# First two token tiles: attention in 128-query blocks instead of 64-query blocks

## The chip, the cores and the metric

The kernel runs on one core of one Trainium2 chip. The core has five engines with queues of their own: TensorE (PE), VectorE (DVE), ScalarE (ACT), GpSimd (POOL) and SyncE (SP), and 16 DMA engines that move data between HBM and the core's SBUF. The metric is the device time of one execution in microseconds.

## The reference

```python
# attention, q k v: (4 batches, 8 heads, 768 positions, 64); mem_k mem_v: (4, 8, 8, 64); chunk 32
for c in range(24):
    k_full = concat([mem_k, k[:, :, max(0, 32*c-16):min(768, 32*c+40)]])      # 8 memory rows + at most 56 rows
    s = q[:, :, 32*c:32*c+32] @ k_full.T / 8
    a = exp(s - max(s)); a = a / (sum(a) + 1e-9)
    out[:, :, 32*c:32*c+32] = a @ v_full                                      # the same rows of v
x = out as (3072 tokens, 512)                                                 # heads side by side
h = x @ w_in;   y = maximum(0.01*h, h) @ w_out                                # w_in 512x2048, w_out 2048x512
h = y @ w_in2;  out = P(h) / (Q(h) + 1e-6) @ w_out2                           # P cubic, Q quadratic
```

The weights arrive as float64, the rest as float32.

## The kernel before

The 3072 tokens go through both layers in six tiles of 512 tokens. A layer's tile is a loop over 16 items `f` of 128 hidden columns: a group of 12 matmuls `hps` (L597: four slices of the contraction times three products of high and low parts), an activation on ACT with a subtraction on DVE (L607 to L610), and a group of 12 matmuls `acc` (L655 in the first layer, L693 in the second). `advance_h` runs `hps` two items ahead of `acc`.

The first layer's weights are loaded and converted while its first tile runs. A half (128 columns of `w_in` or 128 rows of `w_out`, 512 KB as float64) goes through one of three `wr` buffers: `load_w` (SP), `scale_w` (ACT, L133), `join_w` (three DVE instructions, L147 to L154; the last one frees the buffer), `split_w` (ACT, L165) and the low part (DVE, L168). `weights0` does one step of each, twice per item.

Attention of a tile has to be done before that tile's first `hps`. Tiles 2 to 5 use the `wide_*` functions: blocks of 128 queries, transposed by DVE and by DMA through HBM, while matmuls of earlier tiles run. The first two tiles have other functions, `att_*`, with blocks of 64 queries and TensorE for every transpose: `att_a` transposes q (every second block) and k and copies both out of PSUM on ACT; `att_b1` makes the scores and their maximum; `att_e` is the exponential; `att_b2` divides by the sum; `att_c` transposes the probabilities and copies them out in four pieces; `att_d` multiplies by v and splits the result into `xh` and `xl`. The eight blocks of the first tile run at the start, with nothing beside them but loads and the first weights; the exponential follows a subtraction on DVE (L311). The eight blocks of the second tile are put by `attend` into the items of the first tile's first layer; there the exponential takes the maximum as bias and gives the sum (L324).

The order on each engine is the order of the calls in the source: the program is recorded under `tc.manual_schedule()`, and an engine does its instructions in that order. Semaphores are added between engines. A PSUM bank, an SBUF buffer or a DMA semaphore that is used again makes the new user wait for the old one; loads on SP and ACT share eight DMA semaphores in turn, so a load is issued only when the load eight places before it has landed. `psw` is a ring of four PSUM banks for `hps` and attention, `psa` four banks for `acc`, lent to attention during the start.

Of the kernel before, what the change touches and what calls it, by code (L numbers as in the profile page):

```python
# [9 lines left out]
F32 = mybir.dt.float32  # L10
# [7 lines left out]
QB = 64  # L18
# [6 lines left out]
def kernel(  # L25
# [31 lines left out]
    CTX = QB + LCTX + RCTX  # L57
# [4 lines left out]
    assert WIN == SB and QB == 2 * CHUNK  # L62
# [145 lines left out]
    NB = sum(n for _, n in tiles_of[0][:WIDE_FROM]) // QB  # L208
    BPS = S // QB
    tile_of = {}  # L210
    for i, (s0, n) in enumerate(tiles_of[0][:WIDE_FROM]):
        for j in range(s0 // QB, (s0 + n) // QB):
            tile_of[j] = (i, j * QB - s0)

    FIRST = tiles_of[0][0][1] // QB
    spare = [xpool.tile([P, KC, NMAX], F32R, tag=t, name=t) for t in ("xh", "xl")]  # L220
    room = [t[:, n, :].bitcast(F32).rearrange("p (h d) -> p h d", h=H) for t in spare for n in range(KC)]
    rooms = {"k": [kb[0], kb[1]] + room[0:2], "v": [vb[0], vb[1]] + room[2:4], "q": room[4:8]}

    def place(kind, j):
        return j % (4 if j < FIRST else NKV)

    qr, qT, kT, pm = {}, {}, {}, {}
    in_mem = {}

    def load_kv(j, src, mem, kind, spans):  # L230
        bi, blk = divmod(j, BPS)
        t = rooms[kind][place(kind, j)]
        c0 = blk * QB - LCTX
        for row, at, n, is_mem in spans:
            if is_mem:
                if in_mem.get((kind, place(kind, j), row)) != bi:
                    in_mem[kind, place(kind, j), row] = bi
                    nc.sync.dma_start(out=t[row:row + n], in_=mem[bi].rearrange("h p d -> p h d"))  # L238
            else:
                lo, hi = max(c0 + at, 0), min(c0 + at + n, S)  # L240
                row += lo - c0 - at
                nc.sync.dma_start(out=t[row:row + hi - lo], in_=src[bi, :, lo:hi, :].rearrange("h p d -> p h d"))  # L242

    def load_q(j):
        bi, blk = divmod(j, BPS)
        t = rooms["q"][j // 2] if j < FIRST else raw.tile([P, H, D], F32, tag="qr", name="qr", bufs=1)
        nc.sync.dma_start(out=t, in_=q[bi, :, blk * QB:blk * QB + P, :].rearrange("h p d -> p h d"))
        qr[j] = t

    def load_k(j):  # L250
        load_kv(j, k, mem_k, "k", ((0, 0, NM, True), (NM, 0, CTX, False), (NM + CTX, 0, NM, True)))

    def load_qk(j):
        if j >= NB:
            return
        if j % 2 == 0:
            load_q(j)
        load_k(j)

    def load_v(j):  # L260
        if j < NB:
            W = WIN - NM
            load_kv(j, v, mem_v, "v", ((0, 0, NM, True), (NM, 0, W, False),
                                       (SB, CHUNK, W, False), (SB + W, 0, NM, True)))

    def att_bank(j, name):

        if j < FIRST:
            return psa.tile([P, 512], F32, tag="acc", name=name)
        return psw.tile([P, 512], F32, tag="ps", name=name)  # L270

    def att_a(j):
        if j % 2 == 0:
            t = qr.pop(j).rearrange("p h d -> p (h d)")
            ps = psw.tile([P, 512], F32, tag="ps", name="psq")
            for p in range(NP):
                nc.tensor.transpose(ps[:, p * P:(p + 1) * P], t[:, p * P:(p + 1) * P], ident)
            o = tmp.tile([P, NP, P], F32, tag="A", name="qT")
            nc.scalar.mul(out=o.rearrange("p c m -> p (c m)"), in_=ps, mul=scale)
            qT[j] = qT[j + 1] = o  # L280
        t = rooms["k"][place("k", j)].rearrange("p h d -> p (h d)")
        ps = psw.tile([P, 512], F32, tag="ps", name="psk")
        for p in range(NP):
            nc.tensor.transpose(ps[:, p * KW:(p + 1) * KW], t[:KW, p * P:(p + 1) * P], ident[:KW, :KW])
        o = tmp.tile([P, NP, KW], F32, tag="kT", name="kT", bufs=1)
        nc.scalar.copy(out=o.rearrange("p c m -> p (c m)"), in_=ps[:, :NP * KW])
        kT[j] = o

    def att_b1(j):
        blk = j % BPS  # L290
        ps = psw.tile([P, 512], F32, tag="ps", name="pss")[:, :NP * WIN].rearrange("p (c m) -> p c m", c=NP)
        qt, kt = qT.pop(j), kT.pop(j)
        qo = (j % 2) * QB
        for p in range(NP):
            for e in range(2):
                r = slice(e * 64, e * 64 + 64)
                for c in range(2):
                    o = e * 64 + c * CHUNK
                    nc.tensor.matmul(ps[o:o + CHUNK, p, :], qt[r, p, qo + c * CHUNK:qo + (c + 1) * CHUNK],  # L299
                                     kt[r, p, c * KOFF:c * KOFF + WIN], start=True, stop=True)  # L300
        for e in range(2):
            if blk == 0:
                nc.vector.memset(ps[e * 64:e * 64 + CHUNK, :, NM:NM + LCTX], NEG)
# [62 lines left out]

    NCH = P // CHUNK
# [503 lines left out]
```

## Time and profile before

| | us |
|---|---|
| median of 3 runs (1160.58 to 1161.16) | 1160.8 |
| span of the profiled execution, first to last instruction | 1158.6 |
| first `hps` matmul starts (end of the start) | 47.07 |
| first scores of tile 2 on TensorE, in item 14 of the first tile | 156.79 |
| PE busy | 1132.9 (98%) |
| DVE, ACT, POOL busy | 776.2, 637.2, 223.2 |

The page gives the span of the profiled execution and no other time for it; the median of the runs is 2.2 us above that span. In the rows below "busy" of PE is modelled from issue to end of pipelined matmuls, so two matmuls issued 0.23 us apart can each last 0.39 us. In a timeline, the start of the next row is therefore the better measure of what a group costs its engine. `<-` after a bracket names what ended the wait before a row. Shapes with `f32` are float32 matmuls, which the trace records as two instructions each where the operand is not an identity.

### The profile page before, as it was taken

What the parts mean: (1) busy time and instruction counts of PE and PEld (TensorE: products, weight loads), DVE (VectorE), ACT (ScalarE), POOL (GpSimd) and SP (SyncE); (2) the same over time, 40 slices, a digit from 0 to 9 for tenths busy, and PEclk for the clock granted to TensorE, in tenths of its full rate; (3) what the DMA queues carried; (4) which work ended last, traced back from release to release, by engine and by line L of the source; (5) the groups of instructions that cost most, each with busy time, mean ns of one, the idle gap of its engine ahead of it and who ended that gap; (6) DMA issues with size and microseconds to landing.
All of it is one profiled execution on the core that took longest, in us unless ns stands there. A gap on an engine that the chain in (4) does not pass through costs nothing.

```text
span 1158.6 us, 19707 instructions
## 1 busy us (share of the span) xinstructions
PE 1132.9 (98%) x7552; PEld 927.0 (80%) x7552; DVE 776.2 (67%) x1388; ACT 637.2 (55%) x1195; POOL 223.2 (19%) x255
## 2 busy tenths in 40 slices
PE   6799999999999999999999999999999999999998
PEld 4577778888888888888888888888888888888887
DVE  3788865564555645543344888788788788788775
ACT  4677642332233223232345877777777777777765
POOL 0000111232121321130000222222222222222222
PEclk7899999999999999999999999999999999999999
DMA  8677787778777678753342200200200200200001
GB/s 175 165 199 194 182 239 192 204 223 256 205 194 240 195 214 235 200 161 102 99 144 73 92 1 1 73 1 1 73 1 1 73 1 1 73 1 1 37 1 37
DMA packets 148592, 132.00 MB, mean 114 GB/s; under 512 B 63415, under 2 KB 119063, under 8 KB 148499
## 3 DMA queue, kind: packets, MB, share of 16 engines
q1 hardware_dynamic: 143635, 123.30, 37.8%
q0 software_dynamic: 4864, 7.45, 2.7%
q8 instruction: 60, 0.98, 0.4%
q14 instruction: 33, 0.27, 0.1%
HBM read 92.93 MB, written 37.75 MB: 113 GB/s over the span
## 4 chain that ended last, share of the span: by engine, by line
PE 93%; ACT 2%; DMA 2%; DVE 1%; SPq 1%; issue 1%; ACTq 0%; DVEq 0%
PE hps L597 45%; PE acc L693 23%; PE acc L655 22%; PE psx L507 2%; PE pss L465 1%; DMA kb<-in_k_dram 1%; ACT pb L347 1%; SPq L238 1%; DMA wr<-in_moe_w_in_dram 0%; DMA qr<-in_q_dram 0%; SPq L242 0%; PE psx L354 0%; DVE ww L150 0%; PE pss L299 0%; ACT pm L324 0%
## 5 line engine op out<-in xcount | busy, mean ns | idle before, releaser
L633 POOL TENSOR_TENSOR gl<-R,gh 128x512 fp32r<-128x512 f32 x96 | 124.4, 1296 | 503.3 <-ACT gh L632 460.9
L607 ACT ACTIVATE gh<-hps 128x512 fp32r<-128x512 f32 x96 | 57.5, 599 | 295.3 <-PE hps L597 295.2
L610 DVE TENSOR_TENSOR gl<-s,gh 128x512 fp32r<-128x512 f32 x96 | 66.4, 691 | 183.4 <-ACT s L608 180.2
L597 PE MATMUL hps<-xh,wih 128*128 128x512 f32 x384 | 154.1, 401 | 0.9 <-ACT xh L363 0.5
L655 PE MATMUL acc<-gh,woh 128*128 128x512 f32 x384 | 151.4, 394 | 0.0
L597 PE MATMUL hps<-xh,wil 128*128 128x512 f32 x384 | 150.4, 392 | 0.4 <-DVE wil L168 0.4
L597 PE MATMUL hps<-xl,wih 128*128 128x512 f32 x384 | 150.3, 392 | 0.0
L655 PE MATMUL acc<-gh,wol 128*128 128x512 f32 x384 | 149.7, 390 | 0.0
L655 PE MATMUL acc<-gl,woh 128*128 128x512 f32 x384 | 149.5, 389 | 0.0
L693 PE MATMUL acc<-woh,gl 128*128 128x512 f32 x384 | 149.4, 389 | 0.0
L597 PE MATMUL hps<-yh,wih 128*128 128x512 f32 x384 | 149.4, 389 | 0.0
L693 PE MATMUL acc<-woh,gh 128*128 128x512 f32 x384 | 149.4, 389 | 0.0
L597 PE MATMUL hps<-yl,wih 128*128 128x512 f32 x384 | 149.4, 389 | 0.0
L693 PE MATMUL acc<-wol,gh 128*128 128x512 f32 x384 | 149.4, 389 | 0.0
L597 PE MATMUL hps<-yh,wil 128*128 128x512 f32 x384 | 149.4, 389 | 0.0
L430 POOL DMA_DIRECT2D vb<-in_v_dram x128 | 83.7, 655 | 258.3 <-PE psx L507 202.0
L620 ACT ACTIVATE A<-hps 128x512 f32<-128x512 f32 x96 | 57.1, 595 | 113.9 <-PE hps L597 113.8
L636 DVE SCALAR_TENSOR_TENSOR A<-A,small,pb 128x512 f32<-128x512 f32 x96 | 72.0, 750 | 56.5 <-ACT pb L621 56.4
L597 PEld LDWEIGHTS hps<-xh,wih 128*128 128x128 f32 x384 | 72.4, 189 | 17.7 <-ACT xh L363 0.7
L627 DVE SCALAR_TENSOR_TENSOR A<-A,pb 128x512 f32<-128x512 f32 x96 | 66.4, 692 | 30.1 <-ACT pb L640 30.1
L597 PEld LDWEIGHTS hps<-xh,wil 128*128 128x128 f32 x384 | 72.4, 188 | 16.2 <-DVE wil L168 0.8
L655 PEld LDWEIGHTS acc<-gh,wol 128*128 128x128 f32 x384 | 72.1, 188 | 15.5 <-DVE wol L168 0.3
(102 smaller groups left out, 2018.7 us busy)
## 6 DMA issues: line engine op xcount, KB each, us to landing
wr<-in_moe_w_in_dram SPq DMA_DIRECT2D x32, 512.0 KB
wr<-in_moe_w_out_dram SPq DMA_DIRECT2D x32, 512.0 KB
park_dram<-pb SPq DMA_DIRECT2D x16, 512.0 KB
pb<-park_dram SPq DMA_DIRECT2D x64, 128.0 KB
w_dram<-ww SPq DMA_DIRECT2D x32, 256.0 KB
wb<-w_dram SPq DMA_DIRECT2D x32, 256.0 KB
vb<-in_v_dram POOLq DMA_DIRECT2D x118, 56.0 KB, 3.6
kb<-in_k_dram SPq DMA_DIRECT2D x59, 112.0 KB
```

What stands on the lines that cost most here:

```text
L238: nc.sync.dma_start(out=t[row:row + n], in_=mem[bi].rearrange("h p d -> p h d"))
L430: nc.gpsimd.dma_start(out=vw[r + at:r + at + n, c], in_=v[bi, hs, lo:lo + n, :].rearrange("h p d -> p h d"))
L507: nc.tensor.matmul(ps[hh][e * 64:e * 64 + 64, i, c * CHUNK:(c + 1) * CHUNK], vw[r, c, 2 * i + e, :], pt[r, c, 2 * i + e, :], start=True, s ...
L597: nc.tensor.matmul(ps[:, :n], w_[:, ws], x_[:, kk, :], start=(kk == 0 and m == 0), stop=(kk == KC - 1 and m == 2))
L607: nc.scalar.activation(out=gh, in_=ps, func=AF.Prelu, alpha=0.01)
L610: return [lambda: nc.vector.tensor_tensor(out=gl, in0=s, in1=gh.bitcast(F32), op=ALU.subtract)]
L620: nc.scalar.activation(out=A, in_=ps, func=AF.Square)
L627: nc.vector.scalar_tensor_tensor(out=A0, in0=A0, scalar=ONE, in1=U0, op0=ALU.add, op1=ALU.mult)
L633: nc.gpsimd.tensor_tensor(out=gl, in0=R0, in1=gh.bitcast(F32), op=ALU.subtract)
L636: nc.vector.scalar_tensor_tensor(out=A, in0=A, scalar=babs[:, 1:2], in1=U, op0=ALU.mult, op1=ALU.add)
L655: nc.tensor.matmul(acc[i][d][:, :n], w_[:, ws], g_, start=(f == 0 and m == 0), stop=(f == FC - 1 and m == 2))
L693: nc.tensor.matmul(acc[i][s], g_[:, ss], w_, start=(f == 0 and m == 0), stop=(f == FC - 1 and m == 2))
```

## The change

The 64-query functions go. The first two tiles get functions of their own for blocks of 128 queries, four blocks per tile:

- `mid_a` transposes q (4 transposes) and two 64-query windows of k (4 each) and copies them out in three ACT instructions. The second window has a PSUM bank of its own.
- `mid_s` makes the scores of all eight heads into two banks, even heads and odd heads, in the same loop as `wide_s`.
- `mid_p` transposes four slabs of 128x128 and copies them out in one ACT instruction instead of eight for two blocks.
- `mid_x` multiplies by v with contraction over 64 rows instead of 128: 32 matmuls of 32 columns for 128 queries instead of 16 of 64 columns. v lies as it does for the later tiles, heads 0 to 3 in rows 0 to 63 and heads 4 to 7 in rows 64 to 127. `weighted` is the loop of `wide_x`, now shared.
- v of a block comes in 8 loads of 56 KB instead of 4 of 112 KB for the same queries. The first block's v is issued from ACT, memory rows of all later k and of all v from POOL.
- There are three rooms for k and v (two in spare `xh`, `xl` buffers); from the fourth block on all use room 0. The first four q blocks lie in spare weight buffers.
- `plan` puts a block of the second tile into six half-items (two per item): transposes of the probabilities of the block before and of q and k in the first, weighted sum of the block before and scores in the second, then the exponential and the division.

```diff
-    def att_c(j):
-        t, _ = pm.pop(j)
-        t = t.rearrange("p (i h) m -> p i (h m)", h=2)
-        ps = att_bank(j, "pst")[:, :NP // 2 * P]
-        for i in range(NP // 2):
-            nc.tensor.transpose(ps[:, i * P:(i + 1) * P], t[:, i, :], ident)
-        ...
+    room = [(kw, vflat), (spare[0][:, 0], spare[0][:, 1]), (spare[1][:, 0], spare[1][:, 1])]
+    def home(j):
+        return j if j < len(room) else 0
+    def mid_load_v(j):
...
+        eng = nc.sync if j else nc.scalar
...
+        for hh in range(2):
+            hs = slice(4 * hh, 4 * hh + 4)
+            for odd in range(2):
...
+                for n in range(2):
...
+                    eng.dma_start(out=t[row + lo - a0:row + hi - a0, odd, n],
+                                  in_=v[bi, hs, lo:hi, :].rearrange("h p d -> p h d"))
+    def mid_p(j):
+        t, _ = mm.pop(j)
+        t = t.rearrange("p e (i h) m -> p (e i) (h m)", h=2)
...
+        for n in range(4):
+            nc.tensor.transpose(ps[:, n * P:(n + 1) * P], t[:, n, :], ident)
+        nc.scalar.copy(out=pwT, in_=ps)
+    def weighted(j, vt, weight, bank):
+        ps = [bank(j, "psx")[:, :2 * P].rearrange("p (i m) -> p i m", i=2) for hh in range(2)]
+        for i in range(2):
+            for c in range(NCH):
+                for hh in range(2):
+                    r = slice(hh * WIN, hh * WIN + WIN)
+                    for e in range(2):
+                        nc.tensor.matmul(ps[hh][e * 64:e * 64 + 64, i, c * CHUNK:(c + 1) * CHUNK],
+                                         vt[r, c, 2 * i + e, :], weight(r, c, i, e), start=True, stop=True)
...
+        for j in range(FIRST, LAST):
+            u = 1 + 6 * (j - FIRST)
+            if j > FIRST:
+                put(u, lambda j=j: mid_p(j - 1))
+            put(u, lambda j=j: mid_a(j))
+            if j > FIRST:
+                put(u + 1, lambda j=j: mid_x(j - 1), lambda j=j: mid_load_v(j))
+            put(u + 1, lambda j=j: mid_s(j))
+            if j + 1 < LAST:
+                put(u + 1, lambda j=j: mid_load_q(j + 1), lambda j=j: mid_load_k(j + 1))
+            put(u + 2, lambda j=j: mid_e(j))
+            put(u + 3, lambda j=j: mid_n(j))
...
+        mid_x(1)
+        load_w(FC * 2)
+        weights0()
+        mid_a(3)
+        mid_n(2)
+        mid_load_q(FIRST)
+        mid_load_k(FIRST)
+        mid_s(3)
+        mid_p(2)
+        mid_e(3)
+        mid_x(2)
+        weights0()
+        mid_n(3)
+        mid_p(3)
+        mid_x(3)
```

Three places show how the instructions move; line numbers with `+` are those of the changed kernel.

On ACT, at the end of the start before, the third half of the weights (`wr_350`) is scaled ahead of the copy of the last k block:

```order
L363 CAST xh_284<-psx_461 128x4x64
L165 CAST wih_474<-ww_352 128x512
L133 ACTIVATE ww_477<-wr_350 128x512
L286 COPY kT_510<-psk_505 128x416
L319 ACTIVATE pm_83<-pm_83 128x256
```

After the change the third half is `wr_362`, and behind its scaling stand the copies of q and both k windows of the last of four blocks:

```order
L387 CAST xh_348<-psx_440 128x2x128
L387 CAST xh_348<-psx_441 128x2x128
L164 CAST wih_480<-ww_241 128x512
L132 ACTIVATE ww_483<-wr_362 128x512
L299 ACTIVATE qT_496<-psq_491 128x512
L307 COPY pb_82<-psk_498 128x416
L307 COPY pb_82<-psk_504 128x416
```

In both the scaling stands directly ahead of the last k copies; what is behind it is an eighth of the tile's attention before and a quarter now.

On SP before, the loads around that third half (`xh` holds v of blocks 6 and 7 here):

```order
L121 DMA wr_350<-in_moe_w_in_dram 128x4x256
L242 DMA xh_85<-in_v_dram 56x8x64 x2
L124 DMA wr_412<-in_moe_w_out_dram 128x1024
L242 DMA xh_85<-in_v_dram 56x8x64 x2
L121 DMA wr_483<-in_moe_w_in_dram 128x4x256
```

The same place after the change (`xl` is v of the third block, `vb` that of the fourth):

```order
L285 DMA xl_86<-in_v_dram 56x4x64 x8
L247 DMA q0_175<-in_q_dram 128x8x64
L262 DMA kb_80<-in_k_dram 88x8x64 x2
L285 DMA vb_81<-in_v_dram 56x4x64 x8
L120 DMA wr_362<-in_moe_w_in_dram 128x4x256
L123 DMA wr_478<-in_moe_w_out_dram 128x1024
```

The third half has moved behind all of the first tile's v.

On PE in the second tile, between two `hps` and `acc` groups, before (of the groups of twelve, one row stands at each end):

```order
L655 MATMUL acc<-gh,wol 128x512
L342 MATMUL pst<-ident,pm 128x128 x2
L299 MATMUL pss<-kT,qT 32x64 x16
L354 MATMUL psx<-pb,vb 64x64 x8
L597 MATMUL hps<-xh,wih 128x512
```

And after, the transposes in one gap:

```order
L637 MATMUL acc<-gh,wol 128x512
L364 MATMUL pst<-ident,t 128x128 x4
L297 MATMUL psq<-ident,qr 128x128 x4
L306 MATMUL psk<-ident,kb 128x104 x8
L579 MATMUL hps<-xh,wih 128x512
```

Behind that group of twelve, in the next gap, stand the weighted sum of the block before and the scores:

```order
L579 MATMUL hps<-xh,wil 128x512
L379 MATMUL psx<-pm,vb 64x32 x32
L320 MATMUL pss<-pb,qT 32x64 x32
L637 MATMUL acc<-gh,woh 128x512
L637 MATMUL acc<-gl,woh 128x512
```

A block of 128 queries now stands in two gaps between groups of twelve; two blocks of 64 stood in five or six.

## Rows read from the trace of the kernel before

**Rows 1.** Windows by stage: PE, PEld, DVE, ACT, POOL busy, PEclk, DMA share, GB/s.
```profile
0.00:47.07 47.07, 27.93 (x449) 21.60 (x449) 26.27 (x73) 24.15 (x68) 1.59 (x7) 0.78 0.72 155
47.07:156.79 109.72, 106.92 (x820) 84.49 (x820) 92.06 (x184) 74.65 (x206) 10.06 (x16) 0.99 0.77 200
156.79:1158.60 1001.81, 998.03 (x6285) 820.91 (x6284) 657.88 (x1132) 538.40 (x922) 211.56 (x232) 1.00 0.35 103
```

**Rows 2.** Windows of shorter stretches, the same columns; the last is GB/s.
```profile
0.00:13.22 13.22, 7.44 (x105) 5.77 (x109) 4.01 (x14) 4.63 (x9) 1.59 (x7) 1.00 0.72 166
0.00:34.00 34.00, 21.61 (x346) 16.90 (x346) 15.33 (x45) 15.49 (x42) 1.59 (x7) 0.80 0.87 185
...
40.00:44.00 4.00, 2.11 (x20) 1.52 (x20) 3.17 (x10) 2.60 (x10) 0.00 (x0) 0.50 0.07 26
...
200.00:250.00 50.00, 49.98 (x515) 40.55 (x514) 29.07 (x71) 14.40 (x29) 11.31 (x18) 1.00 0.76 208
```

**Rows 3.** Timeline of SP: start, duration, the second load of a weight half.
```profile
13.22 0.39 SPq L121 DMA_DIRECT2D wr<-in_moe_w_in_dram  x1
```

**Rows 4.** Timeline of PE in the start: start, duration, group [wait before it].
```profile
24.80 1.12 PE L354 MATMUL psx<-pb,vb 128*64 128x64 f32 x16
25.85 1.08 PE L299 MATMUL pss<-kT,qT 64*32 64x64 f32 x32
...
40.50 0.66 PE L342 MATMUL pst<-ident,pm 128*128 128x128 f32 x2 [3.36 <-DVE pm L335]
41.09 1.12 PE L354 MATMUL psx<-pb,vb 128*64 128x64 f32 x16
```

**Rows 5.** Groups by line and shape, ACT and DVE: busy us, mean ns | idle before.
```profile
L133 ACT ACTIVATE ww<-wr 128x512 f32<-128x512 f32 x63 | 42.7, 680 | 5.4 <-DMA wr<-in_moe_w_out_dram 3.0 <-DMA w_dram<-ww 2.0 <-DMA wr<-in_moe_w_in_dram 0.4
L286 ACT COPY kT<-psk 128x416 f32<-128x416 f32 x16 | 8.1, 507 | 9.0 <-PE psk L284 9.0
L363 ACT CAST xh<-psx 128x256 fp32r<-128x256 f32 x16 | 6.0, 373 | 4.7 <-PE psx L354 4.6
L279 ACT ACTIVATE qT<-psq 128x512 f32<-128x512 f32 x8 | 4.8, 599 | 10.9 <-PE psq L277 10.9
...
L487 DVE TENSOR_TENSOR t<-t,sm 128x512 f32<-128x512 f32 x16 | 11.1, 692 | 0.6
```

**Rows 6.** DVE timeline: first row of one weight half, first row of the next.
```profile
69.03 0.42 DVE L147 TENSOR_SCALAR ww<-ww 128x512 uint32<-128x512 uint32 x1
...
71.42 0.42 DVE L147 TENSOR_SCALAR ww<-ww 128x512 uint32<-128x512 uint32 x1
```

**Rows 7.** The chain of waits, pieces in order: start, us to the next, what.
```profile
47.07 9.84 PE hps L597 x36
...
108.59 0.44 PE psq L277 x4
109.03 0.36 PE psk L284 x4
...
112.17 0.22 PE pst L342 x2
112.39 2.76 PE hps L597 x12
115.15 0.58 PE pss L299 x32
115.73 0.61 PE psx L354 x16
116.34 2.96 PE acc L655 x12
```

**Rows 8.** The same chain at the later tiles' scores and weighted sums.
```profile
156.86 0.79 PE pss L465 x53
...
183.37 2.72 PE hps L597 x12
186.09 1.30 PE psx L507 x64
```

More of the change, by code (lines that the diff above doesn't have):

```diff
@@ L207 @@
     xt = {}
[L208 to L242, printed above, removed]
@@ L260, in load_v @@
[L260 to L303, printed above, removed]
-            if blk == BPS - 1:
-                o = e * 64 + CHUNK
-                nc.vector.memset(ps[o:o + CHUNK, :, WIN - NM - RCTX:WIN - NM], NEG)
-        mx = tmp.tile([P, NP, 1], F32, tag="mx", name="mx")
-        nc.vector.tensor_reduce(out=mx, in_=ps, op=ALU.max, axis=AX.X, negate=True)
-        if j < FIRST:
-            t = mall[:, j % 2]
-            nc.vector.tensor_tensor(out=t, in0=ps, in1=mx.to_broadcast([P, NP, WIN]), op=ALU.add)
-            pm[j] = (t, None)
-        else:
-            pm[j] = (ps, mx)
@@ new lines, in mid_bank, with mid_a @@
+    def mid_bank(j, name):
+        if j < FIRST:
+            return psa.tile([P, 512], F32, tag="acc", name=name)
+        return psw.tile([P, 512], F32, tag="ps", name=name)
+    def mid_a(j):
+        t = mq.pop(j)
+        ps = psw.tile([P, 512], F32, tag="ps", name="psq")
+        for p in range(NP):
+            nc.tensor.transpose(ps[:, p * P:(p + 1) * P], t[:, p * P:(p + 1) * P], ident)
+        o = tmp.tile([P, NP, P], F32, tag="A", name="qT")
+        nc.scalar.mul(out=o.rearrange("p c m -> p (c m)"), in_=ps, mul=scale)
+        mqT[j] = o
+        t = room[home(j)][0]
+        for n in range(2):
+            ps = psw.tile([P, 512], F32, tag="ps", name="psk")[:, :NP * KW]
+            for p in range(NP):
+                f = n * H * D + p * P
+                nc.tensor.transpose(ps[:, p * KW:(p + 1) * KW], t[:KW, f:f + P], ident[:KW, :KW])
+            nc.scalar.copy(out=kwT[:, n * NP * KW:(n + 1) * NP * KW], in_=ps)
@@ new lines, in mid_e @@
+    def mid_e(j):
+        t, ps, mx = mm[j]
+        sm = None
+        if j < FIRST:
+            nc.scalar.activation(out=t, in_=t, func=AF.Exp)
+        else:
+            sm = tmp.tile([P, 2, NP, 1], F32, tag="sm", name="sm", bufs=3)
+            for e in range(2):
+                for p in range(NP):
+                    nc.scalar.activation(out=t[:, e, p, :], in_=ps[e][:, p, :], func=AF.Exp, bias=mx[:, e, p, :],
+                                         accum_out=sm[:, e, p, :])
+        mm[j] = (t, sm)
@@ new lines, in mid_n @@
+    def mid_n(j):
+        t, sm = mm[j]
+        t = t.rearrange("p e n m -> p (e n) m")
+        if sm is None:
+            sm = tmp.tile([P, H, 1], F32, tag="sm", name="sm", bufs=3)
+            nc.vector.tensor_reduce(out=sm, in_=t, op=ALU.add, axis=AX.X)
+        else:
+            sm = sm.rearrange("p e n m -> p (e n) m")
+        nc.vector.tensor_scalar_add(sm, sm, 1e-9)
+        nc.vector.reciprocal(out=sm, in_=sm)
+        nc.vector.tensor_tensor(out=t, in0=t, in1=sm.to_broadcast([P, H, WIN]), op=ALU.mult)
@@ new lines @@
+        for j in (1, 2):
+            mid_load_q(j)
+            mid_load_k(j)
+            mid_load_v(j)
+            if j == 1:
+                load_w(FC * 2)
+        mid_load_q(3)
+        mid_a(0)
+        mid_load_k(3)
+        mid_s(0)
+        mid_e(0)
+        scale_w(FC * 2)
+        mid_a(1)
+        mid_n(0)
+        mid_s(1)
+        mid_p(0)
+        mid_e(1)
+        mid_x(0)
+        mid_load_v(3)
+        load_w(FC * 2)
+        join_w(FC * 2)
+        scale_w(FC * 2)
+        mid_a(2)
```

270 lines of the change are left out of this document (108 added, 162 removed).

## The prediction

> **What bounds the kernel now.** I read the windows by stage first, then the chain of waits, then the timelines of the stages that the change touches. The windows cut the span in three [rows 1]. From 156.79 us on, PE is busy 998.03 of 1001.81 us and none of its instructions change, so I carry that stage over whole. From 47.07 to 156.79 us the first tile's matmuls run with the second tile's attention between them: PE 106.92 of 109.72 us, and DVE, which converts the weights, 92.06. Up to 47.07 us the first tile's attention runs alone, and PE is busy 27.93 us only: there the end is set by loads (185 GB/s over the first 34 us, then 26 GB/s at 40 to 44 us [rows 2]) and, after them, by a ladder of handovers between PE, ACT and DVE, as in the 3.36 us that PE waits for the division at 40.50 us [rows 4]. So the change has two prices, one for each of the first two stages, and they need not have the same sign.
>
> **The start: removed and added.** ACT and DVE save work: two blocks of 64 need eight copies of probabilities, one block of 128 one copy of 512 columns, which I take as the q copy's 0.60 us [rows 5]. That saving lies on engines busy about half of this stage [rows 1], and is worth nothing by itself. What counts is when the last block starts and how long its ladder is.
>
> When it starts. In the changed order ACT scales the third weight half directly ahead of the last block's q and k copies, and SP issues that half behind all of v. In the order before, two of the eight v blocks were still behind the third half. I count what is loaded up to and with it: q 1024 KB, k 1376, v 1760, memory rows 384, three halves 1536, together 6080 KB (6.23 MB); before, 5504 KB. The start moves 185 GB/s [rows 2], so 6.23 MB are through at 33.7 us at the earliest. Landing lags: the first weight half and what was issued ahead of it are 1840 KB (1.88 MB), the load that has to wait for it goes out at 13.22 us [rows 3], and by then 13.22 x 166 = 2.19 MB had moved [rows 2]. With those 0.31 MB (1.7 us) added the third half lands at 35.4 us. I take 35.0, nearer to the measured lag; bounds 33.7 and 38, the upper for a queue that runs dry between the small loads.
>
> How long the ladder is from there. PE's granted clock was 0.50 at 40 to 44 us [rows 2], after PE had waited 3.36 us, and the last block meets the same: PE has nothing to do while ACT waits for the weight. At that level (1.2 GHz) the weighted sum took 1.05 us (24.80 to 25.85) [rows 4] against 0.61 at the full one [rows 7], a factor 1.72. Steps, in order: scaling 0.68, q copy 0.60 and two k copies of 0.51, less 0.3 for their overlap, 2.0 [rows 5]; scores 0.79 x 1.72 = 1.36 [rows 8]; transposes of the third block's probabilities, two pairs of 0.59, 1.18 [rows 4]; their copy 0.60; the third block's weighted sum 1.30 x 1.72 = 2.24 [rows 8]; `xh` 0.37 [rows 5]; two low parts on DVE, of 256 columns like `xh` and taken at its 0.37, 0.74; then, ahead of the last division on DVE, one weight half, 71.42 - 69.03 = 2.39 [rows 6]; the division 1.75 (sum and multiplication at 0.69 each [rows 5], two short ones); transposes 1.18, copy 0.60, weighted sum 2.24, `xh` 0.37. That is 17.0, and 17.3 with a dozen handovers. At the full clock the three weighted sums and scores and the transposes shrink by 3.8 in all: 13.5.
>
> So `hps` starts at 35.0 + 17.3 = 52.3 us instead of 47.07: **+5.2**. Ends: 33.7 + 13.5 = 47.2 (+0.1) and 38 + 17.3 = 55.3 (+8.2).
>
> The loads come in smaller pieces: v in 56 KB instead of 112 KB. The later tiles also load v in 56 KB pieces, and at 200 to 250 us 208 GB/s moved beside them [rows 2], so I charge nothing for the size; if I am wrong it is inside the bound of 38. The Trainium skill, "DMA: Bandwidth & Descriptors", section "Bandwidth", says the opposite: transfers under 64 KB are mostly overhead, with 138 GB/s given for 64 KB. By that figure, as an estimate, the 1.80 MB of v would take 13.0 instead of 9.7 us, and the start would come out 3.3 us later still.
>
> **The stage behind it.** PE's transposes are the same in number (4 of q, 8 of k, 4 of probabilities for 128 queries), on both sides at the same rows [rows 7]: nothing. Scores for 128 queries go from 2 x 0.58 [rows 7] to 0.79 [rows 8], weighted sums from 2 x 0.61 to 1.30: -0.29 a block, -1.2 for four. The weighted sum has twice the matmuls at half the columns and gains nothing by it.
>
> Gaps: a group of twelve takes 2.72 us undisturbed [rows 8], 2.96 behind scores and weighted sum and 2.76 behind a transpose [rows 7], so a gap costs 0.14 on average. I count 22 gaps before and 10 after: -1.7.
>
> Stalls: 31 groups of 2.72 are 84.3; the first three lose 9.84 - 8.16 = 1.7 to the half clock, which I keep; eight blocks cost 4 x 0.44 + 8 x (0.36 + 0.22 + 0.58 + 0.61) = 15.9; 22 gaps 3.1. Of 109.7 that leaves 4.7 us of stalls, in which PE waits for ACT and DVE. ACT loses seven of its eight copies of probabilities a block, DVE one of two multiplications and two short instructions, so they should shrink; but they won't vanish: the second bank of the scores is the bank of the `hps` group just before it, and the next `hps` needs the bank whose low part DVE has still to read. I take 2.5 of 4.7: -2.2. Ends: all gone, -4.7, and 2 us more than before, +2.0.
>
> Together -1.2 - 1.7 - 2.2 = **-5.1**, between -7.6 and -0.9.
>
> **Sum.** 1158.6 + 5.2 - 5.1 = 1158.7 us of span; the median of the runs shown is 2.2 us above the span of the profiled execution, so 1160.9. Both terms are sure in sign and I trust neither to better than 2 us; that they cancel is chance.
>
> **Rivals.** First, the start loses little (faster): the third half lands at 34 us and the clock is back at full in the middle of the ladder; 34 + 15 = 49, +2; with the stage at -6 the time is 1156.8. For it: the mean granted clock of the start is 0.78 [rows 1], so PE was at the full level for a good part of it. Against: 0.50 at 40 to 44 us, in the stretch most like the new ladder [rows 2, 4].
>
> Second, DVE sets the stage's pace (slower). It is busy 92.06 of 109.72 us now; with about as much in a stage of 104.6 it would be 88%. Its order has the low parts of the weighted sum, on which a PSUM bank waits, behind four or five weight instructions, and the eight exponentials on ACT in one piece stand ahead of the weight's high part that DVE's next low part needs. If DVE falls behind PE by more than the slack that `hps` has on that bank, a few tenths of a us, every block pays: then only scores and gaps stay, -1.5 with the stalls 1.4 longer, and the time is 1160.8 + 5.2 - 1.5 = 1164.5. It decides as soon as PE waits over 1.5 us a block. For it: before, PE already waited for ACT and DVE. Against: the PE windows show 97% busy [rows 1].
>
> Third, the loads run dry (slower): the third half lands at 38 us; +8.2 - 5.1, so 1163.9. Only eight loads are out at a time, and eight of 56 KB are 448 KB, 2.4 us at 185 GB/s: about a landing's lag. Against: the pieces are mixed with loads of 176 to 512 KB. The skill's rule above would end here, by its own figure at about 1164.
>
> **Chances.** Forecast (both terms within 2 us of mine) 0.45, first rival 0.27, second 0.16, third 0.12. A change of 0.2% (2.3 us) is about what a measurement of this kernel can tell. Of the forecast's 0.45, 0.33 lie within it, 0.06 on either side; of the first rival 0.22 are faster, 0.05 within; of the second 0.12 slower and 0.04 within; of the third 0.1 slower, 0.02 within. So faster 0.28, same 0.44, slower 0.28. Forecast's own range 1158 to 1164; the range for 8 in 10 is 1155.5 to 1166.
>
> **What would show it.** Right: ACT waits at the scaling ahead of the last q copy, for the DMA of the third half, until about 35 us; first `hps` near 52 us; granted clock 0.5 around 40 to 50 us; first later-tile scores about 104 to 105 us after the first `hps`, with half as many groups of 2.9 us. Wrong: `hps` before 49 us, or the stage as long as before, or PE waits in it for PSUM banks of `psx` and `pss` of over 1 us a block. If the time from the first later-tile scores to the end differs from 1001.8 by over 1 us, the premise that the rest is untouched has failed.

## The result

| | before | after |
|---|---|---|
| median | 1160.7 us (4 runs) | 1167.6 us (4 runs, 1166.9 to 1169.4) |
| span of the profiled execution | 1158.6 | 1167.6 |
| first `hps` | 47.07 | 57.10 |
| from there to the first scores of the third tile | 109.72 | 108.89 |
| from there to the end | 1001.81 | 1001.61 |

The change makes the kernel slower: the ratio of the times is 1.0065, 95% interval 1.0051 to 1.0079, 6.9 us between the medians. The profiled execution is the longest of its four (1169.4), so the 9.0 us between the two spans is some 2 us more than the typical loss. They split as 10.0 in the start, -0.8 in the stage behind it (from the first `hps` to the first scores of the third tile) and -0.2 in the rest. The windows by stage answer to [rows 1], those of shorter stretches to [rows 2] (same columns; PEclk, DMA share and GB/s stand last):

```profile
0.00:57.10 57.10, 29.55 (x577) 23.09 (x577) 23.20 (x57) 17.60 (x35) 18.31 (x38) 0.84 0.69 149
57.10:165.99 108.89, 103.99 (x948) 84.91 (x948) 90.72 (x173) 68.87 (x179) 15.06 (x26) 0.97 0.69 190
165.99:1167.60 1001.61, 997.70 (x6285) 820.59 (x6284) 657.73 (x1132) 538.46 (x922) 214.15 (x235) 1.00 0.35 103
0.00:34.00 34.00, 19.68 (x366) 14.90 (x367) 12.11 (x32) 10.99 (x21) 18.31 (x38) 1.00 0.83 162
25.00:35.00 10.00, 8.05 (x150) 6.45 (x149) 5.84 (x14) 3.89 (x8) 0.00 (x0) 1.00 0.77 141
40.00:45.00 5.00, 2.67 (x68) 1.87 (x68) 1.33 (x4) 2.12 (x5) 0.00 (x0) 0.50 1.04 273
```

In the start the loads moved 162 GB/s over 34 us where [rows 2] had 185, and the DMA engines were busy 0.83 of it. In the stage PE is busy 104.0 us instead of 106.9, and the time is still there: PE waits more.

**The start.** SP's timeline after the change (start, duration; x8 is a row of eight loads), then ACT's and PE's:

```profile
22.44 4.84 SPq L285 DMA_DIRECT2D xl<-in_v_dram  x8
27.58 0.39 SPq L247 DMA_DIRECT2D q<-in_q_dram  x1
28.09 2.10 SPq L262 DMA_DIRECT2D kb<-in_k_dram  x2
30.29 5.83 SPq L285 DMA_DIRECT2D vb<-in_v_dram  x8
36.16 0.40 SPq L120 DMA_DIRECT2D wr<-in_moe_w_in_dram  x1
```

```profile
40.47 0.66 ACT L132 ACTIVATE ww<-wr 128x512 f32<-128x512 f32 x1 [5.67 <-DMA wr<-in_moe_w_in_dram]
```

```profile
31.66 2.03 PE L379 MATMUL psx<-pm,xh 64*64 64x32 f32 x64 [0.73 <-ACT pm L365]
...
42.07 1.62 PE L320 MATMUL pss<-pb,qT 64*32 64x64 f32 x64 [6.02 <-ACT pb L307]
43.62 1.11 PE L364 MATMUL pst<-ident,t 128*128 128x128 f32 x4
45.47 2.03 PE L379 MATMUL psx<-pm,xl 64*64 64x32 f32 x64 [0.73 <-ACT pm L365]
52.89 1.09 PE L364 MATMUL pst<-ident,t 128*128 128x128 f32 x4 [5.39 <-DVE t L357]
54.71 2.03 PE L379 MATMUL psx<-pm,vb 64*64 64x32 f32 x64 [0.73 <-ACT pm L365]
57.10 0.80 PE L579 MATMUL hps<-xh,wih 128*128 128x512 f32 x1 [0.36 <-ACT xh L387]
```

The third weight half goes out at 36.16 us, behind eight loads that took 5.83 us to issue. ACT waits 5.67 us for it, PE 6.02 us behind ACT. Then the ladder runs 16.6 us, with 5.39 us in it in which PE waits for a division.

This execution is the latest of its kind. Six of the kernels below (experiments 7 to 10, 12 and 13) start in the same order. In their profiles ACT scales that half at 37.5 to 40.2 us, and the first `hps` stands at 54.2 to 56.8, in each 16.6 us behind the scaling. So the start costs 7 to 10 us by execution, the 10.0 above are the high end, and what varies is when the half lands.

**The stage behind.** PE's rows at its three long waits:

```profile
110.60 1.23 PE L306 MATMUL psk<-ident,kb 104*128 104x104 f32 x8
112.80 0.50 PE L579 MATMUL hps<-xh,wih 128*128 128x512 f32 x1 [0.97 <-ACT pm L365]
...
132.32 0.94 PE L306 MATMUL psk<-ident,kb 104*128 104x104 f32 x8
134.23 0.50 PE L579 MATMUL hps<-xh,wih 128*128 128x512 f32 x1 [0.97 <-ACT pm L365]
...
150.43 0.63 PE L364 MATMUL pst<-ident,t 128*128 128x128 f32 x4 [2.83 <-DVE t L357]
```

The step from `psk` to `hps` takes 2.20 and 1.91 us at these places, 0.66 at the first block (71.41 to 72.07). What ACT did before it copied the probabilities (`pm`), and what SP did before that:

```profile
109.55 0.69 ACT L132 ACTIVATE ww<-wr 128x512 f32<-128x512 f32 x1 [2.88 <-DMA wr<-in_moe_w_in_dram]
...
112.19 0.56 ACT L365 COPY pm<-pst 128x512 f32<-128x512 f32 x1
```

```profile
97.93 4.49 SPq L285 DMA_DIRECT2D vb<-in_v_dram  x8
102.46 0.67 SPq L247 DMA_DIRECT2D qr<-in_q_dram  x1
103.17 1.05 SPq L262 DMA_DIRECT2D kb<-in_k_dram  x2
104.33 1.11 SPq L120 DMA_DIRECT2D wr<-in_moe_w_in_dram  x1
```

Eleven loads in a row, 6.3 us, stand ahead of a weight half; ACT waits for the half; the copy of the probabilities is queued behind it, with four more ACT instructions between; PE's bank behind the copy. At the second place ACT's wait for the half is 2.75 us. The third wait, for the last block's division (L357), has weight instructions ahead of it on DVE:

```profile
148.56 0.68 DVE L167 TENSOR_TENSOR wol<-ww,woh 128x512 fp32r<-128x512 f32 x1
...
149.59 0.69 DVE L357 TENSOR_TENSOR t<-t,sm 128x512 f32<-128x512 f32 x1
```

I summed PE's timeline of the stage by kind of group, from the first row of a group to the first of the next (a wait counts with the group before it):

| us | hps | acc | psq | psk | pss | pst | psx | sum |
|---|---|---|---|---|---|---|---|---|
| before | 50.43 | 40.39 | 1.73 | 3.40 | 5.05 | 2.49 | 6.23 | 109.72 |
| after | 50.43 | 41.82 | 1.73 | 5.46 | 3.47 | 1.70 | 4.28 | 108.89 |

Scores (`pss`), transposes of probabilities (`pst`) and weighted sums (`psx`) became 4.3 us cheaper; `psk` and `acc`, which the new waits are counted with, became 3.5 us dearer. The equal sums of `hps` hide one more loss: the first three groups took 11.15 us (57.10 to 68.25) where before they took 9.68 (47.07 to 56.75), since PE stayed longer at the half clock, and the other `hps` groups gained as much.

### The profile page after: what moved, and what is told of

Same layout as the page of the kernel before. It is cut to its first block, busy times and chain, and to the rows that moved or that the text cites. A ratio compares the mean times of both kernels' runs of the same rounds, so it can differ in the third digit from the quotient of the medians.

```text
span 1167.6 us, 20228 instructions
## 1 busy us (share of the span) xinstructions
PE 1131.2 (97%) x7808; PEld 928.6 (80%) x7808; DVE 771.6 (66%) x1361; ACT 624.9 (54%) x1135; POOL 247.5 (21%) x298
## 4 chain that ended last, share of the span: by engine, by line
PE 91%; DMA 3%; ACT 2%; DVE 2%; issue 1%; SPq 1%; ACTq 0%; DVEq 0%
PE hps L579 44%; PE acc L675 22%; PE acc L637 20%; PE psx L379 2%; DMA wr<-in_moe_w_in_dram 1%; PE pss L475 1%; ACT t L343 1%; DMA xl<-in_k_dram 1%; DVE ww L149 1%; DMA xh<-in_v_dram 0%; DMA vb<-in_v_dram 0%; SPq L262 0%; ACT ww L132 0%; DVE wol L167 0%; PE pst L364 0%
## 5 line engine op out<-in xcount | busy, mean ns | idle before, releaser
L602 ACT ACTIVATE A<-hps 128x512 f32<-128x512 f32 x96 | 57.1, 595 | 114.0 <-PE hps L579 114.0
L579 PEld LDWEIGHTS hps<-xl,wih 128*128 128x128 f32 x384 | 72.8, 190 | 14.6 <-DVE xl L388 0.2
```

What stands on the lines that cost most here:

```text
L579: nc.tensor.matmul(ps[:, :n], w_[:, ws], x_[:, kk, :], start=(kk == 0 and m == 0), stop=(kk == KC - 1 and m == 2))
L602: nc.scalar.activation(out=A, in_=ps, func=AF.Square)
```

## The experiments

Times are medians; the kernel before ran beside each group at 1160.5 to 1160.6. Edits are to the changed kernel unless said otherwise.

**1. The third half ahead of the fourth block's v.**
```diff
         mid_x(0)
+        load_w(FC * 2)
         mid_load_v(3)
-        load_w(FC * 2)
```


> One edit: the load of the third weight half is issued ahead of the eight loads of the fourth block's v instead of behind them. Theory A (the landing of the third half, at 40.4 us in the changed kernel, sets the end of the start): the load goes out at about 30.3 instead of 36.2 us, lands at 34 to 35, and with the ladder of 16.6 us measured in the changed kernel the first hps starts at 51 to 52 instead of 57.1; time 1161 to 1163 against 1167.6. Rival B (the half only shares the lateness of all the loads; v of the fourth block then comes too late for its weighted sum, or the q and k copies wait for their own loads): hps moves by less than 2 us, time 1165.5 or more.

Measured: the half is issued at 31.00 us and scaled at 36.42, first `hps` at 53.29, 3.8 us earlier. The time is 1167.2 (1.0058, 1.0044 to 1.0072), not told apart from the changed kernel's 1167.6 and what rival B had. Theory A comes within 1.3 us for the start (against the 54.2 to 56.8 of the other executions the gain is 0.9 to 3.5 us) and fails for the total: in its profile the stage took 111.9 us, 3.0 more, and 2.5 of them are two groups of twelve behind waits, which took 4.54 and 3.87 us instead of 2.9 (granted clock 0.62 and 0.74 in them).

**2. The third half ahead of the third block's v.**
```diff
             mid_load_k(j)
+            if j == 2:
+                load_w(FC * 2)
             mid_load_v(j)
...
-        load_w(FC * 2)
```


> One edit: the load of the third weight half is issued ahead of the third block's v already (the run before had it behind that, and ahead of the fourth block's v). Theory A (landing of the half plus a ladder of 16.6 to 16.9 us): the half lands by 30 us, ACT's scaling waits for no load and stands at 34 to 35 us, first hps at 49.5 to 51.5; what is left to 47.1 is the longer ladder. Rival B (k of the fourth block or v of the third, which then land later, take its place): hps at 53 or later. Time by A 1159 to 1163.5, spread by whether the clock falls in the stage behind.

Measured: 1164.6 (1.0038, 1.0025 to 1.0051), first `hps` at 51.79. ACT and PE there:

```profile
33.93 0.70 ACT L132 ACTIVATE ww<-wr 128x512 f32<-128x512 f32 x1
```

```profile
47.58 1.08 PE L364 MATMUL pst<-ident,t 128*128 128x128 f32 x4 [5.40 <-DVE t L357]
51.79 0.79 PE L579 MATMUL hps<-xh,wih 128*128 128x512 f32 x1 [0.36 <-ACT xh L387]
```

ACT no longer waits for a load, and `hps` is 2.4 to 5.3 us earlier than in the seven executions with the order of the change (54.2 to 57.1). It is 0.3 us outside what A expected, and 4.7 us later than before. So of the 7 to 10 us, 2.4 to 5.3 are the late half and 4.7 stay without it, because the ladder is longer: 17.9 us from the scaling to `hps`, where before it was 47.07 - 35.36 = 11.7, by ACT's row of that kernel:

```profile
35.36 0.69 ACT L133 ACTIVATE ww<-wr 128x512 f32<-128x512 f32 x1
```

**3. The same, and the last division ahead of a weight half on DVE.**
```diff
         mid_x(2)
-        weights0()
         mid_n(3)
+        weights0()
         mid_p(3)
```


> The third half loaded as in the run that had it ahead of the third block's v (first hps at 51.79), and one edit more: at the end of the start the last block's division stands ahead of a weight half on DVE instead of behind it. Theory A (with the loads out of the way what is left over 47.1 us is the longer ladder, 17.9 us from ACT's scaling to the first hps, and in it the 5.4 us that PE waits for that division are a weight half's 2.5 us and the low parts too many): the division comes 2.4 to 3.1 us earlier, hps at 48.6 to 49.4, time 1161.5 to 1163. Rival B (the weights that now come later stop the first hps or acc groups): hps at 49 as well, but the time gains under 1 us against 1164.6.

Measured: 1163.5 (1.0027, 1.0018 to 1.0036), `hps` at 50.66; the wait for the division falls from 5.40 to 2.98 us, and `hps` moves by 1.1 only, in part since ACT's scaling stood 0.7 us later in this execution. The gain in time, 1.1 us, lies between A and B; the intervals of the two runs overlap, so it is not clear of noise.

**4. v of the second to fourth block issued by GpSimd.**
```diff
-        eng = nc.sync if j else nc.scalar
+        eng = nc.sync if j >= FIRST else nc.gpsimd if j else nc.scalar
```


> One edit: v of the second to fourth block is issued by GpSimd instead of SyncE, in the same 56 KB pieces. Theory A (the loads run slowly because only eight loads of SyncE and ACT are out at a time and the pieces are small): with a second queue beside it the first 34 us move 180 GB/s or more (162 in the changed kernel), the third half lands by 31 us, hps starts at 46 to 50, time 1157 to 1161. Rival B (56 KB pieces are slow in the DMA engines themselves): rate stays 155 to 168 GB/s, v lands late and PE waits for it in the weighted sums, hps at 52 or later, time 1163 or more.

Measured: 1174.2 (1.0120, 1.0103 to 1.0137). Neither: 172 GB/s, the half issued at 22.61, but PE waited 7.50 us for memory rows of k that stood on GpSimd behind the second block's v; `hps` at 57.83. It tells nothing of small pieces, and something of that queue (last section).

**5. v of the second to fourth block in pieces of 28 KB.**
```diff
-                    eng.dma_start(out=t[row + lo - a0:row + hi - a0, odd, n],
-                                  in_=v[bi, hs, lo:hi, :].rearrange("h p d -> p h d"))
+                    for g in range(0, 4, 2 if 0 < j < FIRST else 4):
+                        ge = g + (2 if 0 < j < FIRST else 4)
+                        eng.dma_start(out=t[row + lo - a0:row + hi - a0, odd, n, g:ge],
+                                      in_=v[bi, 4 * hh + g:4 * hh + ge, lo:hi, :].rearrange("h p d -> p h d"))
```


> The changed kernel with v of the second to fourth block in pieces of 28 KB, 16 a block instead of 8, the same bytes. Theory A (in the start the loads run slowly because eight at a time are out, and small ones hold few bytes): the first 34 us move under 150 GB/s instead of 160 to 170, the third half is issued at 40 us or later (33 to 36.2 so far), hps at 60 or later, time 1171 or more. Rival B (the DMA engines are the limit, whose work is by bytes or rows, the same in both): 155 to 170 GB/s, third half issued at 33 to 37, hps at 54.5 to 58, time 1166 to 1169.

Measured: 1178.1 (1.0155, 1.0141 to 1.0169), `hps` at 65.22. SP's rows, then a window:

```profile
24.81 8.71 SPq L287 DMA_DIRECT2D xl<-in_v_dram  x16
...
35.57 8.93 SPq L287 DMA_DIRECT2D vb<-in_v_dram  x16
44.55 0.39 SPq L120 DMA_DIRECT2D wr<-in_moe_w_in_dram  x1
```

```profile
25.00:35.00 10.00, 7.02 (x143) 5.60 (x144) 3.94 (x9) 3.40 (x6) 0.00 (x0) 1.00 0.47 92
```

Theory A. In a row a load takes SP 0.54 to 0.56 us at 28 KB and 0.61 to 0.73 at 56 KB (4.84 and 5.83 for eight); before the change it was 0.82 at 112 KB:

```profile
24.05 3.29 SPq L242 DMA_DIRECT2D vb<-in_v_dram  x4
```

Four times the bytes cost half as much again, so the rate follows the size of the pieces. Over the first 34 us it was 136 GB/s here, 161 to 170 in the seven executions with 56 KB, and 185 before; from 25 to 35 us it was 92, 141 to 170, and 214. The DMA engines were busy 0.47 of that stretch here, so their capacity, rival B, is not what limited it. Whether the price of a load is that of eight under way (an estimate: 8 x 0.56 = 4.5 us each) or SP's own work for it (0.39 us where it waits for nothing) was not told apart.

**6. The start of before, the second tile in blocks of 128.** All of `att_*` stays for the first tile, `mid_*` and `plan` serve the second.

> First tile in blocks of 64 as in the kernel before, second tile in blocks of 128 as after the change. Theory A (the start alone makes the change slower, and the second tile gains 0.8 us and no more): first hps at 47.1 us, from there to the first scores of the third tile 108 to 109 us, time 1159 to 1160.5 against 1160.7 before. Rival B (the second tile would gain the forecast 5.1 us, and lost it only because the late start shifted the weight loads against it): that stage 104 to 106 us, time 1155 to 1157. Rival C (the second tile is itself the loss): time over 1162.

Measured: 1161.6 (1.0011, 1.0002 to 1.0020), `hps` at 46.78, stage 110.27. The time is between A and C, and B falls: the second tile does not gain with an early start either (110.27 against 109.72). The same three waits are there (2.8 for the division, twice 0.97 for the copy).

**7. The start after the change, the second tile in blocks of 64.** The mirror of the last one.

> First tile as after the change, second tile in blocks of 64 as before. Theory A (the change's price is the sum of two parts, 1.0 us for the second tile, measured alone, and the rest for the start): time 1165.5 to 1167.5, first hps at 54.5 to 57.8, stage 109 to 110.5. Rival B (with a late start the old second tile is better or worse off than the new one): time under 1164.5 or over 1168.5.

Measured: 1170.4 (1.0086, 1.0072 to 1.0099), `hps` at 54.53, stage 110.92. Rival B: the new start alone costs 10.0 us, of which its profile shows 7.5 ahead of the first `hps` and 1.2 in the stage behind it. With the late start the new second tile is 2.8 us better than the old one, with the early start 1.0 worse. The parts don't add up, and what couples them stays open.

**8. v of the second tile issued by GpSimd.**
```diff
-        eng = nc.sync if j else nc.scalar
+        eng = nc.gpsimd if j >= FIRST else nc.sync if j else nc.scalar
```


> One edit: the v loads of the second tile are issued by GpSimd instead of SyncE. Theory A (SyncE issues eight v loads per block, about 4.5 us, ahead of the next weight halves, so ACT waits 2.9 and 2.8 us at 109.55 and 130.98 us for a weight and PE behind it): these two waits shrink below 0.5 us, PE's two waits of 0.97 us behind them vanish, the last one of 2.8 us for the division shrinks; stage 105 to 107.5 instead of 109.0 us, time 1164 to 1166. Rival B (DVE and ACT are simply full there, and the load's lateness is covered): stage within 0.5 us of 109.0, time 1167 to 1168.

Measured: 1168.6 (1.0068, 1.0053 to 1.0083), stage 108.81. ACT's longest wait for a weight falls from 2.9 to 1.4 us and PE's wait at the fourth block is gone, but the third block waits for memory rows behind v on GpSimd:

```profile
107.36 0.55 PE L306 MATMUL psk<-ident,kb 104*128 104x104 f32 x4 [0.41 <-DMA kb<-in_mem_k_dram]
109.04 0.55 PE L306 MATMUL psk<-ident,kb 104*128 104x104 f32 x4 [1.13 <-ACT pb L307]
```

One wait was taken away and another made, and the one for the division stayed (2.9 us). By its stage that is rival B; the time is 0.6 us above B's.

**9. The last block's transposes and weighted sum one half-item later.**
```diff
-                put(u + 4, lambda j=j: mid_p(j))
-                put(u + 5, lambda j=j: mid_x(j))
+                put(u + 5, lambda j=j: mid_p(j))
+                put(u + 6, lambda j=j: mid_x(j))
```


> One edit: in the second tile the last block's transposes of the probabilities and its weighted sum stand one half-item later. Theory A (PE's wait of 2.83 us for the division of that block, the same in every kernel with the new second tile so far, is there because only three groups of twelve lie between its scores and its transposes, 8.2 us, while maximum, exponential, weights and division need 11): the wait disappears, the stage from the first hps to the first scores of the third tile is 105 to 106.5 us instead of 109, time 1163 to 1165. Rival B (DVE is simply behind; the wait moves to the next hps or to the first hps of the second tile): stage 108 or more, time 1166.5 or more.

Measured: 1173.3 (1.0105, 1.0086 to 1.0124), stage 115.9. The wait for the division is gone and a longer one stands behind it; ACT and PE:

```profile
156.10 0.67 ACT L132 ACTIVATE ww<-wr 128x512 f32<-128x512 f32 x1 [4.20 <-DMA wr<-in_moe_w_out_dram]
...
159.67 0.58 ACT L365 COPY pm<-pst 128x512 f32<-128x512 f32 x1
```

```profile
160.30 0.97 PE L379 MATMUL psx<-pm,vb 64*64 64x32 f32 x28 [3.88 <-ACT pm L365]
```

One half-item later, ACT's copy is queued behind one more scaling, and that one waits 4.20 us for a half that SP had behind v and the third tile's loads. Two groups of twelve behind long waits took 5.42 and 4.98 us in this profile, the slowest of its six. Rival B, and worse than it had.

**10. v of a block in two parts, four loads each, with two weight halves between.**
```diff
-        for hh in range(2):
+        for hh in part:
...
-                put(u + 1, lambda j=j: mid_x(j - 1), lambda j=j: mid_load_v(j))
+                put(u + 1, lambda j=j: mid_x(j - 1))
+                put(u + 3, lambda j=j: mid_load_v(j, (0,)))
+                put(u + (3 if j + 1 == LAST else 5), lambda j=j: mid_load_v(j, (1,)))
```


> One edit: in the second tile the eight v loads of a block are issued four and four, each with two weight halves between, instead of eight together ahead of the q and k loads. Theory A (the weight half that stands behind eleven loads in a row makes ACT wait, and behind ACT the copy of the probabilities and PE's bank): ACT's waits of 2.9 and 2.8 us for a weight shrink below 1 us, PE's excess of 1.5 and 1.3 us ahead of the hps of the third and fourth block falls below 0.5 each, stage 106 to 107.5 instead of 109, time 1164 to 1166. Rival B (the copy stands behind DVE's and ACT's own work): excess stays, stage 108.5 to 109.5.

Measured: 1174.2 (1.0121, 1.0107 to 1.0136), stage 115.2. The mechanism of A is right: ACT's longest wait for a weight is 0.5 us, and the steps from `psk` to `hps` are 0.96 and 0.66. But v is late now:

```profile
111.47 0.30 PE L379 MATMUL psx<-pm,vb 64*64 64x32 f32 x4
114.03 2.10 PE L379 MATMUL psx<-pm,vb 64*64 64x32 f32 x60 [2.25 <-DMA vb<-in_v_dram]
```

**11. The start of before with 9 and 10.**

> First tile as before, second tile in blocks of 128 with the two edits of the runs beside it (last block later, v in two parts). Theory A: start at 46.8 to 47.1 us, stage 104 to 106.5 us instead of 110.3 (with the edits left out) and 109.7 (kernel before), time 1155.5 to 1158, below the kernel before. Rival B (the waits move on): stage 108.5 or more, time 1160 or more.

Measured: 1164.5 (1.0032, 1.0020 to 1.0044), stage 111.7: rival B, with waits for v (4.0 us) and for the copy (1.7).

**12. The last block's division one weight half earlier on DVE.**
```diff
-            put(u + 3, lambda j=j: mid_n(j))
+            put((u + 2, 1) if j + 1 == LAST else u + 3, lambda j=j: mid_n(j))
...
                 weights0()
+                wide((2 * c + 1, 1))
```


> The changed kernel with one edit: the division of the second tile's last block stands, on DVE, one weight half earlier. Theory A (PE's wait of 2.83 us is DVE's order alone, not the loads): the wait falls to 0.5 us or less, and no clock falls behind it; stage 105.5 to 106.5 us instead of 109, time 1164 to 1165.5. Rival B (ACT's copy of the transposes or the later low part of the activation takes its place): stage above 108.

Measured: in the profile the wait is gone and the stage takes 105.87, as A had it; the time is 1167.2 (1.0061, 1.0049 to 1.0073). The profiled execution was the second fastest of six that lie between 1165.6 and 1170.0. Shown is that the wait is DVE's order; the time is not told apart from the changed kernel's 1167.6, so what the edit is worth by itself is inconclusive.

**13. 12, and v by GpSimd behind q, k and memory rows of the next block.**
```diff
-        eng = nc.sync if j else nc.scalar
+        eng = nc.gpsimd if j >= FIRST else nc.sync if j else nc.scalar
...
-                put(u + 1, lambda j=j: mid_x(j - 1), lambda j=j: mid_load_v(j))
+                put(u + 1, lambda j=j: mid_x(j - 1))
...
                 put(u + 1, lambda j=j: mid_load_q(j + 1), lambda j=j: mid_load_k(j + 1))
+            if j > FIRST:
+                put(u + 1, lambda j=j: mid_load_v(j))
```


> The changed kernel, second tile: v by GpSimd as in an earlier run, but behind q, k and memory rows of the next block (that run had PE wait for those), and the division earlier as in the run beside this. Theory A (the three waits of the stage are loads behind loads on one queue, twice, and DVE's order, once; there is no other limit): all three go, stage 103 to 104.5 us, time 1161 to 1163.5 with the start as changed. Rival B (what DVE and ACT have to do for the weights fills the stage, so that waits taken away in one place come back in another): stage 106 or more, with a wait in a new place.

Measured: 1167.1 (1.0055, 1.0039 to 1.0070), stage 105.15 in the profile, which is of the fastest of six (1164.0 to 1169.3). The three waits are gone, one of 2.5 us for the last block's v has come.

**14. The start of before with 13.**

> Start as before, second tile in blocks of 128 with the two edits of the run beside this (v by GpSimd behind the next block's q and k, division earlier). Theory A: first hps at 47, stage 103 to 105 us, time 1154.5 to 1157: 4 to 6 us less than before. Rival B: stage 107 or more, time 1158.5 or more.

Measured: 1158.6 (0.9981, 0.9973 to 0.9990), stage 109.19: faster than before for the first time, and behind the first `hps` PE waits long in one place only, at the last weighted sum (waited for, us in total, times, longest); the group of twelve behind it took 5.28 us instead of 2.9:

```profile
PE psx L539 <- DMA vb<-in_v_dram: 3.0, 2, 1.9
```

**15. 14, with four of the last block's eight v loads on SP again.**
```diff
+            eng = nc.sync if j + 1 == MLAST and hh else first
```


> As the last run with the start of before, and one edit more: of the last block's eight v loads four go through SyncE again. In that run's profile all three old waits of the stage were gone, and a new one stood at the last weighted sum: PE waited 1.88 and 1.17 us for v, with the following group at half clock. Theory A (GpSimd issues its loads too slowly, and that is all that is left): this wait goes, stage 103 to 105 us instead of 109.2, time 1153.5 to 1156. Rival B (four loads more ahead of the third tile's loads and the last weight halves on SyncE make a wait there): stage 106.5 or more, time 1156.5 or more.

Measured: **1153.1** (0.9936, 0.9922 to 0.9949), 0.6% faster than before. Its waits of PE, and its window of the stage:

```profile
PE hps L785 <- ACT xh L363: 0.5, 1, 0.5
PE pss L481 <- ACT s L796: 0.4, 1, 0.4
```

```profile
46.82:150.03 103.21, 102.81 (x949) 84.46 (x949) 90.09 (x172) 69.55 (x178) 32.18 (x52) 0.98 0.78 211
```

DVE does what it did in the slow kernels (90.1 us), in 103.2 us: the amount of its work was not the bound. Experiment 6 has the same start and the same blocks without these edits to the orders: 1161.6 us, stage 110.27. The edits are worth 8.5 us.

**16. Both tiles in blocks of 128, with 3, 13 and 15.**

> Both tiles in blocks of 128: the start with the third half ahead of the third block's v and the division ahead of a weight half, the second tile as in the run beside this. Theory A (start and stage add up): hps at 50 to 51.5, stage 103 to 105.5, time 1157 to 1160.5. Rival B (a second tile without slack is hit harder by a later start): stage 107 or more, time 1161 or more.

Measured: 1157.0 (0.9970, 0.9960 to 0.9981), `hps` at 49.42, stage 103.51. Faster than before too, and 3.9 us slower than with the old start: even mended, the new start costs that, 2.6 of it ahead of the first `hps` in the two profiles.

## Why the prediction was wrong

Both terms failed, on the same side, and each came out near the number of one of the rivals.

**"The third half lands at 35.4 us. I take 35.0."** This is the step that failed in the start. It landed at 40.4 in the profiled execution, and at 37.5 to 40.2 in the six others with this order. The rate was taken from [rows 2], 185 GB/s of a kernel with v in 112 KB; with 56 KB it was 162 over 34 us, and with 162 the prediction's own sum gives 38.4 us for its 6.23 MB and 40.1 with its lag of 1.7. Experiment 5 shows that the rate falls with the number of loads at the same bytes. "I charge nothing for the size" rested on 208 GB/s in a stretch where 512 KB weight halves ran beside the small v loads, and where GpSimd issued those and not SP; it was the wrong row to lean on. The bound of 38, meant for this, was up to 2.4 us short.

The rule of the Trainium skill that I had set aside ("DMA: Bandwidth & Descriptors", section "Bandwidth", 138 GB/s for 64 KB, measured there for loads that GpSimd issued) came nearer than my row. The 3.3 us that I had worked out by it would have put the first `hps` at 55.6, within the 54.2 to 57.1 measured. Its figure is close to the 141 GB/s of this execution and below the 144 to 170 of the six others; the 92 GB/s with halved pieces fall as it says.

**"How long the ladder is from there", 17.3 us**: right, 40.47 to 57.10 is 16.6, at the half clock as assumed (the granted clock is 0.50 at 40 to 45 us). That column does not tell all: from 31 to 34 us it reads 1.00, yet the same weighted sum took 2.03 us at 31.66 as at 45.47, against 1.14 in the stage (94.03). By the times of its matmuls PE was at the half level there too, and so it was in the ladder of experiment 2, where the column reads 1.00. The first rival, which argued from its mean of 0.78, leaned on a reading that a matmul's duration can check. Experiment 2 confirms it from the other side: without the wait for the load the ladder takes 17.9 us, and the first `hps` is still 4.7 us later than before.

**"I take 2.5 of 4.7" us of stalls.** This is the step that failed in the stage. They did not shrink by 2.2; the three new waits alone are 1.5 + 1.3 + 3.0 us (2.20 and 1.91 against 0.66, and an `acc` group with the wait for the division at 5.72 against 2.72). I looked for them in the PSUM banks of `psx` and `pss`; they were in the orders of SP, ACT and DVE: a weight half behind eleven loads, a copy behind a scaling, a division behind weights. Experiment 10 takes the first two away, 12 the third, 15 all of them (with the start of before), and then the stage takes 103.2, 1.4 less than the 104.6 forecast. A second term was too small: the first three groups lose 3.0 us to the half clock, not the 1.7 that I kept (by the same count 1.5 before, and 1.6 to 3.0 in the seven executions with the new start). Without the waits (5.8) and that (1.5) the stage would have become 8.1 us cheaper, a little more than the lower end of -7.6. So the scores, the gaps and the old stalls did shrink, and the saved work was there to be had.

**"The rest 1001.8 unchanged"**: 1001.6. Right.

**The rivals.** "DVE sets the pace" had about the right size (only -1.5 of the stage left; measured -0.8) and the wrong cause: DVE is as busy in the kernel of 1153.1, and only one of the three waits stands in its order. "The loads run dry" had the right mechanism (+8.2; measured +7 to +10). I gave them 0.16 and 0.12 as if one excluded the other. They lie in different stages: together, by their own numbers, 1160.8 + 8.2 - 1.5 = 1167.5, against 1167.6 measured. That it agrees to 0.1 us is luck, since neither part did. But the sum was in no chance and beyond the range's upper end of 1166.

What stays open: the parts alone cost 1.0 and 10.0 us, the whole 6.9 (experiments 6 and 7), and executions of kernels with the new start scatter over 2 to 7 us where the kernel before has 3. Why the half lands up to 3 us apart in kernels with the same order of loads stays open too.

## What to carry to other kernels

Count loads, not only bytes: where a queue is full, a row of small loads delays whatever is issued behind it by its number, so the load that something waits for goes ahead of them. A saving on an engine reaches the end only if each engine's order lets it: look at what is queued ahead of each instruction that PE needs, and whether that can itself wait for a load. Rivals in different stages can all come true: add them before setting the range.

## What the runs showed of the hardware

- Loads in a row went out on SP every 0.54 to 0.56 us at 28 KB, 0.61 to 0.73 at 56 KB and 0.82 at 112 KB in the start, with eight under way at most.
- GpSimd was slower at it in experiment 4: eight loads of 56 KB went out between 14.93 and 27.90 us, 1.6 us each, with waits between them for which the trace names nothing:

```profile
17.68 0.65 POOL L285 DMA_DIRECT2D xh<-in_v_dram  x1 [1.06 <-issue]
21.75 1.29 POOL L285 DMA_DIRECT2D xh<-in_v_dram  x2 [3.43 <-issue]
```

- After a wait of PE of 2 to 3 us the granted clock fell to the half level in some executions and not in others: the group of twelve behind the division took 2.95 us after the change and 3.87 to 4.35 in experiments 1, 2, 6 and 8 (granted clock 1.00 against 0.65 to 0.74). At the first `hps` it stayed at the half level for 5.7 us after the change (57.10 to 62.84, granted clock 0.50) and 3.1 before (47.07 to 50.17, 0.52).
